# Two pairs of heads share one group of value products; first weights and the planner's costs changed

## The chip, the cores and the metric

The kernel runs on one core of one Trainium2 chip. The metric is the device time of one execution in microseconds. Before the change three runs gave 741.05, 739.51 and 741.62 us, so the median is 741.05.

## What is computed

Attention over 4 batches, 8 heads, 768 positions and 64 columns a head, followed by a gated feed-forward layer over all 3072 tokens. A query sees the 96 positions up to itself and the first 8 positions of its batch; a bias that grows with the distance is added to the scores.

```python
scores = scale * q @ k.T + bias            # per batch and head, 768 x 768
scores = where(is_global | is_local, scores, -1e9)
a = exp(scores - max(scores)); a = a / (sum(a) + 1e-9)
x = (a @ v), heads side by side            # 3072 x 512
out = ((x @ w_a) * (x @ w_b)) @ w_out      # 512 -> 1536 twice, product, 1536 -> 512
```

## The kernel before

**Units.** The 24 blocks of 128 queries are cut into eight units of 4, 2, 3, 3, 3, 3, 3 and 3 blocks. While PE does the feed-forward layer of one unit (`moe`), the attention of the next unit is made beside it (`attention`; for unit 0 `first`, for unit 1 `second`). Attention writes x, the layer's input, transposed: four chunks of 128 rows, one for each pair of heads.

**The feed-forward layer.** Every factor is split into a high and a low half, and a product is three matmuls: high by high, high by low, low by high. For each of twelve slices f of the 1536 columns, `proj` makes two such products into the banks p0 and p1 (L990, four chunks of x each; 384 columns wide in a unit of three blocks), the two are multiplied (L1029) and split (hh, hl), and `back` adds the product with the third weight to one accumulator a block (acc, L1008, 512 columns).

**Attention of units 2 to 7.** Heads are taken in pairs. For each head `split` makes the scaled query's halves qh and ql and the key's halves in kk. A block's scores are two matmuls, qh and ql, into one PSUM bank (L915); banks psS and psT took turns. DVE reads the bank, adds the bias and finds the maximum (L617), ACT takes the exponential (L633), DVE the sum and its reciprocal, ACT or DVE scales (L665, L667). DVE transposes the probabilities in squares of 32 by 32 into a staging tile in wm (L709), and when the pair is complete 16 small DMAs, on the queues of SP and ACT, put the squares in their places in pf (`swap`). Then PE multiplies pf by the values v: matmuls of 64 by 128, one group for each pair, into a bank pa (`values`, L742), and `result` copies pa to x. One row of L742 in PE's order stands for two matmuls of the trace. There are four such groups in a unit, 24 in units 2 to 7. pf has one buffer, so a pair's squares can land only when the group of the pair before is through.

**Units 0 and 1.** Here `quad` does two blocks of a pair of heads: a scaled query qs (L772 on ACT or L774 on DVE), scores (L789), softmax, transposes on PE (L692) that ACT or DVE copies to pf, and the same `values`.

**Weights.** The weights come as 24 pieces of 768 KB (`load_w`), two for each slice f, in a packed form of 64 bits a number. DMAs on SP's queue bring them to wr; ACT (L461, L498) and DVE (L468, L478, L488, L507) turn each into a float in wm; a copy (L419, L421) writes the high half wt, a subtraction (L429) the low half.

**The order.** No order is written by hand. Every step is an op with a due time, a cost on each engine that may do it, and the buffers that it reads and writes. `Schedule.order` plays the program through: at each moment an engine that is free takes the ready op with the earliest due time for which its buffers are free. `Schedule.search` repeats this with due times shifted at random for the ops due before the end of unit 1, and keeps a trial that ends sooner. The order of every engine, and of the loads on SP's queue, is what comes out. An engine then runs its instructions strictly in that order, each waiting by semaphores for what it needs.

Of the kernel before, what the change touches and what calls it, by code (L numbers as in the profile page):

```python
# [13 lines left out]
F32 = mybir.dt.float32  # L14
F32R = mybir.dt.float32r
# [8 lines left out]
B, H, S, D = 4, 8, 768, 64  # L24
DM, DFF = 512, 1536
P = 128
NB = S // P
NCC = DM // P
# [11 lines left out]
CHUNKS = 12  # L40
SQ = 32

SHORT = PAIRED
OLD = ()

START = 52000
WLEAD = 6000
# [6 lines left out]
SPARE = 200.0  # L54
# [3 lines left out]


TRIES = 400  # L60
SHARE = 0.03
SPREAD = 4000.0
# [82 lines left out]
MAXQ = max(p.nb for p in PLANS[1:]) * P  # L145
# [69 lines left out]
class Schedule:  # L215
# [22 lines left out]
    def search(self, limit, tries, share, spread):  # L238


        rnd = random.Random(1)
        ops = [op for op in self.ops if op.due < limit]
        dues = {op.index: op.due for op in ops}
        best = self.order(ops, dues)[1]
        for _ in range(tries):
            trial = dict(dues)
            for op in ops:
                if rnd.random() < share:
                    trial[op.index] += rnd.gauss(0.0, spread)
            end = self.order(ops, trial)[1]  # L250
            if end < best:
                best, dues = end, trial
        return self.order(self.ops, {op.index: dues.get(op.index, op.due) for op in self.ops})

    def order(self, ops, dues):
# [11 lines left out]
        out = []  # L267
        now = 0.0
        port = 0.0

# [29 lines left out]
        while len(out) < len(ops):  # L300
            started = True
            while started:
                started = False
                for e in free:
# [19 lines left out]
                    out.append(op)  # L324
                    free[e] = now + op.costs[e]
# [27 lines left out]
        return out, now  # L353
# [21 lines left out]
class Fast:  # L375
# [61 lines left out]
    def load_w(self, f, due):  # L437
# [3 lines left out]
        for g in range(2):  # L441
# [12 lines left out]
                due,  # L454
# [109 lines left out]
    def split(self, u, h, due, raw):  # L564
# [8 lines left out]
        ql = self.sbuf([P, MAXQ], F32R, "ql", "ql" + n, 2)  # L573
# [157 lines left out]
    def values(self, due, pl, blocks, v, probs, pa):  # L731


        nc = self.nc

        def emit(e):
            for i in blocks:
                slots = pl.vslot[i]
                for c, slot in enumerate(slots):
                    for s in range(2):  # L740
                        v0 = (s * pl.nv + slot) * D
                        nc.tensor.matmul(  # L742
                            pa[D * s : D * s + D, i * P : i * P + P],
                            v[:, v0 : v0 + D],
                            probs[s, i][1](c),
                            start=c == 0,
                            stop=c == len(slots) - 1,
                        )

        reads = [v] + [probs[s, i][0] for s in range(2) for i in blocks]  # L750
        n = sum(len(pl.vslot[i]) for i in blocks)
        self.plan.op(due, emit, reads, [pa], pe=n * 218 + 290, spare=SPARE if pl.late else 0.0)

    def quad(self, u, c, j, due, raw, v, pa, homes):
# [64 lines left out]
        self.values(due, pl, blocks, v, probs, pa)  # L819
        return pa  # L820

    def first(self, end):
# [14 lines left out]
        loads = [self.fetch_first(c, -1e6 + 2 * c) for c in range(NCC)]  # L837
# [36 lines left out]

    def result(self, u, c, due, pa, x):
# [11 lines left out]
    def attention(self, u, start, end):  # L887
        nc, pl, op = self.nc, PLANS[u], self.plan.op

        x = [(self.raw0, WIDE + c * MAXQ) for c in range(2)]  # L890
        x += [(self.sbuf([P, MAXQ], F32, f"x{c}", f"x{u}_{c}"), 0) for c in range(2, NCC)]
        if u < PAIRED:
            self.second(x, start, end)
            return x
        step = (end - start) / H
        for c in range(NCC):
            probs = {}
            v = self.fetch_v(u, c, start + (2 * c + 1) * step - LOADLEAD)
            pf = self.sbuf([P, CHUNKS * P], F32, "pf", f"pf{u}_{c}", 1)
            slot = 0  # L900
            old = u == SHORT and c in OLD
            for s in range(2):
# [4 lines left out]
                for i in range(pl.nb):  # L907
# [3 lines left out]
                    ps = self.bank(("psS", "psT")[not old and (pl.nb * h + i) % 2], "ps" + n)  # L911
# [37 lines left out]
            pa = self.bank("psA", f"pa{u}_{c}")  # L949
            self.values(due, pl, range(pl.nb), v, probs, pa)  # L950
            self.result(u, c, due, pa, x)
# [116 lines left out]
    def run(self):  # L1068
# [20 lines left out]
        order, end = self.plan.search(t2, TRIES, SHARE, SPREAD)  # L1089
# [376 lines left out]
```

## Time and profile before

| what | value |
|---|---|
| median of three runs | 741.05 us (739.51 to 741.62) |
| profiled execution | 739.72 us, of which the profile's span is 737.9 |
| mean granted TensorE clock | 0.994 |
| busy time of PE, DVE, ACT | 715.4, 480.0, 348.8 us |
| value products (L742), 640 matmuls | 43.7 us busy, 2.9 idle before them |
| scores of units 2 to 7 (L915), 288 matmuls | 77.9 us busy, 0.5 idle before them |
| weights loaded | 24 times 768 KB on SP's queue |

PE is TensorE's matmuls, PEld its weight loads, DVE VectorE, ACT ScalarE, SP SyncE. Busy times of PE overlap: a matmul starts before the one ahead of it is through, and its end is modelled. The distance between the starts of two matmuls therefore says more of PE's pace than the length of one. A row of the timeline gives the start, the time until the end of the last matmul in it, engine, line, what is written and read, the shape and the number of instructions; in brackets stands idle time ahead of it and what ended it. PEclk is the granted clock, 1.00 being full speed.

### The profile page before, as it was taken

To read this page: it belongs to the slowest core of one execution; us is meant where nothing else is said; L and a number is where in the kernel's file an instruction comes from. 1 tells how busy PE (TensorE), PEld (TensorE's weight loads), DVE (VectorE), ACT (ScalarE), POOL (GpSimd) and SP (SyncE) were. 2 spreads that over 40 slices of the span, in tenths; PEclk is the share of its full clock that TensorE was granted. 3 is DMA by queue.
4 is the path that set the end of the run, shared out by engine and by line. 5 is a ranking of instruction groups with operands and counts; after the bars stand their busy time and mean duration, and the time that the engine had idled before them with its cause. 6 is when DMAs were issued, how large, how long until landed. Compare 5 with 4: busy or idle time off the path is not lost.

```text
span 737.9 us, 12581 instructions
## 1 busy us (share of the span) xinstructions
PE 715.4 (97%) x4344; PEld 640.1 (87%) x4344; DVE 480.0 (65%) x1574; ACT 348.8 (47%) x891; POOL 8.9 (1%) x28
## 2 busy tenths in 40 slices
PE   5789999999999999999999999999999999999996
PEld 4567877889988999999999999999999999899996
DVE  5999999958956776287744878268672876321111
ACT  6999967556335353254424544154432544331112
POOL 1000000000000000000000000000000000000000
PEclk9999999999999999999999999999999999999999
DMA  7898211123533234124231443214341242110001
GB/s 282 345 339 326 82 32 33 35 85 110 142 106 113 84 98 116 44 83 110 74 116 44 108 122 96 73 61 107 88 128 55 81 127 62 47 44 0 1 1 47
DMA packets 38520, 74.58 MB, mean 101 GB/s; under 512 B 8496, under 2 KB 21040, under 8 KB 38448
## 3 DMA queue, kind: packets, MB, share of 16 engines
q1 hardware_dynamic: 29232, 65.03, 27.6%
q10 hardware_dynamic: 9216, 8.66, 4.6%
q8 instruction: 36, 0.59, 0.3%
q14 instruction: 36, 0.29, 0.1%
HBM read 50.07 MB, written 6.29 MB: 76 GB/s over the span
## 4 chain that ended last, share of the span: by engine, by line
PE 92%; DVE 4%; ACT 2%; DMA 1%; issue 0%; DVEq 0%; ACTq 0%; SPq 0%
PE p L990 54%; PE acc L1008 27%; PE pa L742 5%; PE ps L915 4%; PE ps L789 2%; DVE t L617 1%; PE pt L692 1%; DMA v<-qkv 0%; DMA nv<-ns 0%; DMA raw<-qkv 0%; DVE kk L429 0%; DVE t L667 0%; ACT kk L419 0%; ACT xh L419 0%; ACT wr L498 0%
## 5 line engine op out<-in xcount | busy, mean ns | idle before, releaser
L990 PE MATMUL p<-xh,wt 128*128 128x384 f32 (+2 forms) x1488 | 418.3, 338 | 1.1 <-DVE wt L429 0.6
L990 PEld LDWEIGHTS p<-xh,wt 128*128 128x128 f32 x1488 | 270.3, 188 | 15.3 <-issue 3.4
L990 PE MATMUL p<-xl,wt 128*128 128x384 f32 (+2 forms) x816 | 270.1, 341 | 0.3 <-DVE xl L429 0.3
L1008 PE MATMUL acc<-wt,hh 128*128 128x512 f32 x576 | 202.5, 394 | 0.0
L990 PEld LDWEIGHTS p<-xl,wt 128*128 128x128 f32 x816 | 153.9, 189 | 10.1 <-issue 1.0
L1008 PEld LDWEIGHTS acc<-wt,hh 128*128 128x128 f32 x576 | 108.2, 188 | 20.5 <-issue 1.3
L1029 DVE TENSOR_TENSOR raw<-p,raw 128x384 f32<-128x384 f32 (+2 forms) x96 | 52.9, 551 | 96.6 <-PE p L990 93.1
L1008 PE MATMUL acc<-wt,hl 128*128 128x512 f32 x288 | 113.1, 393 | 0.0
L633 ACT ACTIVATE t<-t,sm 128x232 f32<-128x232 f32 (+2 forms) x120 | 56.5, 472 | 93.9 <-DMA pf<-wm 77.6
L419 ACT COPY raw<-p 128x384 f32<-128x384 f32 (+2 forms) x84 | 39.9, 475 | 104.1 <-PE p L990 101.5
L1008 PEld LDWEIGHTS acc<-wt,hl 128*128 128x128 f32 x288 | 54.2, 188 | 7.6
L429 DVE TENSOR_TENSOR hl<-raw,hh 128x384 fp32r<-128x384 f32 (+2 forms) x95 | 52.1, 548 | 12.7 <-ACT hh L419 12.0
L617 DVE CUSTOM_DVE_ANT_0 t<-ps,rel 128x232 f32<-128x232 f32 (+1 forms) x100 | 38.1, 397 | 25.6 <-PE ps L915 23.2
L419 ACT CAST hh<-raw 128x384 fp32r<-128x384 f32 (+2 forms) x69 | 35.5, 515 | 39.2 <-DVE raw L1029 33.0
L742 PEld LDWEIGHTS pa<-pf,v 128*64 128x64 f32 x640 | 35.5, 138 | 13.0 <-issue 7.4
L742 PE MATMUL pa<-pf,v 128*64 128x128 f32 x640 | 43.7, 280 | 2.9 <-ACT pf L419 1.3
L633 ACT ACTIVATE wm<-wm,sm 128x232 f32<-128x232 f32 (+2 forms) x72 | 34.0, 472 | 23.8 <-DVE sm L617 20.1
L429 DVE TENSOR_TENSOR kk<-raw,kk 64x348 fp32r<-64x348 f32 (+1 forms) x90 | 41.6, 463 | 2.8
L915 PE MATMUL ps<-kk,ql 128*128 128x232 f32 (+2 forms) x144 | 39.4, 275 | 0.0
L915 PE MATMUL ps<-kk,qh 128*128 128x232 f32 (+2 forms) x144 | 38.5, 270 | 0.5 <-DVE sm L617 0.4
L665 ACT ACTIVATE wm<-wm,sm 128x232 f32<-128x232 f32 (+2 forms) x58 | 27.5, 478 | 23.3 <-DVE sm L655 21.0
L709 DVE STREAM_TRANSPOSE wm<-wm 128x256 f32<-128x256 f32 (+1 forms) x72 | 29.6, 414 | 6.7 <-ACT wm L665 5.7
(87 smaller groups left out, 666.8 us busy)
## 6 DMA issues: line engine op xcount, KB each, us to landing
wr<-wts SPq DMA_DIRECT2D x24, 768.0 KB, 10.8
raw<-qkv SPq DMA_DIRECT2D x24, 366.0 KB, 3.1
raw<-qkv SPq DMA_DIRECT2D x24, 314.0 KB, 2.9
v<-qkv SPq DMA_DIRECT2D x16, 384.0 KB, 3.1
out<-o SPq DMA_DIRECT2D x23, 256.0 KB, 2.1
pf<-wm SPq DMA_DIRECT2D x96, 48.0 KB, 2.0
pf<-wm ACTq DMA_DIRECT2D x96, 48.0 KB, 2.0
v<-qkv SPq DMA_DIRECT2D x16, 256.0 KB, 2.7
```

The costliest lines, as they stand in the source:

```text
L419: self.nc.scalar.copy(out(), src())
L429: lambda e: self.engine(e).tensor_sub(out(), a(), b()),
L617: lambda e, j=j, o=o, w=w, neg=neg: nc.vector.tensor_tensor_reduce(t[:, o : o + w], ps[:, o : o + w], neg[:, :w], -(2.0 ** -(h + 1)), 3.0e ...
L633: lambda e, j=j, o=o, w=w: nc.scalar.activation(t[:, o : o + w], t[:, o : o + w], AF.Exp, bias=sm[:, j : j + 1], scale=-1.0, accum_out=sm[ ...
L665: nc.scalar.mul(t[:, o : o + w], t[:, o : o + w], r)
L709: nc.vector.transpose(dst, src)
L742: nc.tensor.matmul(pa[D * s : D * s + D, i * P : i * P + P], v[:, v0 : v0 + D], probs[s, i][1](c), start=c == 0, stop=c == len(slots) - 1,)
L789: nc.tensor.matmul(ps[s][:, o : o + w], qs[r, q0 + m * P : q0 + m * P + P], raw[r, kc : kc + w], start=True, stop=True,)
L915: nc.tensor.matmul(ps[:, :w], q[:, i * P : i * P + P], kk[:, k0 : k0 + w], start=m == 0, stop=m == 1,)
L990: nc.tensor.matmul(p[:, :T], wt(), b[:, b0 : b0 + T], start=c == 0 and n == 0, stop=c == NCC - 1 and n == 2,)
L1008: nc.tensor.matmul(acc[i][:, :], hs[:, i * P : i * P + P], wt(), start=f == 0 and n == 0, stop=f == NF - 1 and n == 2,)
L1029: lambda e, asb=asb, pb=pb: nc.vector.tensor_mul(asb[:, :T], pb[:, :T], asb[:, :T]),
```

## The change

**Pairs joined.** `values` takes a list of pairs, and `attention` hands it two at a time. So a unit of 2 to 7 has two groups in place of four, each with twice the matmuls; the first pair writes the bank psA, the second psT. psT is thus no longer free for scores, and all scores of these units go to psS. pf has two buffers, and x's second half (chunks 2 and 3) lies in pf's buffers where it had tiles of its own; it is taken only behind the unit's first group. ql has one buffer where it had two. `result` of both pairs comes behind the joined group.

**First weights sooner.** The loads of the two pieces of f = 0, and those of the first unit's queries, keys and values, get due times that interleave them. On SP's queue stood, behind the first pair's loads, raw_1, v_1, raw_2, v_2, raw_3, v_3 and only then the weights; now stands the first piece of weights, raw_1, v_1, the second piece, raw_2, v_2, raw_3, v_3, and further weights.

**The planner.** `order` also adds up the time that PE waits beyond 1.3 us in one place, doubled and at most 1.3 us a place, and `search` minimises the sum of this and the end. It makes 1200 trials in place of 400, and in each shifts fewer due times (1% in place of 3%) by more (8 us in place of 4). It reorders nothing by a rule; but every order of units 0 and 1, and what follows from it, may differ.

```diff
+JOINT = 2
+EARLY = -60000
+LOAD = 4000
+IDLE = 1300.0
+FINE = 2.0
-TRIES = 400
-SHARE = 0.03
-SPREAD = 4000.0
+TRIES = 1200
+SHARE = 0.01
+SPREAD = 8000.0
...
 def search(self, limit, tries, share, spread):
-        best = self.order(ops, dues)[1]
+        best = self.order(ops, dues)[1:]
...
-            end = self.order(ops, trial)[1]
-            if end < best:
-                best, dues = end, trial
+            found = self.order(ops, trial)[1:]
+            if sum(found) < sum(best):
+                best, dues = found, trial
...
 def order(self, ops, dues):
...
+                    if e == "pe":
+                        fine += min(max(now - free[e] - IDLE, 0.0) * FINE, IDLE)
...
 def load_w(self, f, due):
-                due,
+                EARLY + (2 * g + 1) * LOAD if f == 0 else due,
                 lambda e, f=f, g=g, raw=raw: nc.sync.dma_start(...),
...
 def split(self, u, h, due, raw):
-        ql = self.sbuf([P, MAXQ], F32R, "ql", "ql" + n, 2)
+        ql = self.sbuf([P, MAXQ], F32R, "ql", "ql" + n)
...
-    def values(self, due, pl, blocks, v, probs, pa):
+    def values(self, due, pl, blocks, groups):
         def emit(e):
-            for i in blocks:
+            for v, probs, pa in groups:
+                for i in blocks:
...
+        for v, probs, pa in groups:
+            reads += [v] + [probs[s, i][0] for s in range(2) for i in blocks]
+            writes.append(pa)
+        n = len(groups) * sum(len(pl.vslot[i]) for i in blocks)
+        self.plan.op(due, emit, reads, writes, pe=n * 218 + 290, ...)
...
 def first(self, end):
-        loads = [self.fetch_first(c, -1e6 + 2 * c) for c in range(NCC)]
+        loads = [self.fetch_first(c, EARLY + 2 * c * LOAD) for c in range(NCC)]
...
+    def probs32(self, name):
+        return self.sbuf([P, CHUNKS * P], F32, "pf", name, JOINT)
...
 def attention(self, u, start, end):
-        x += [(self.sbuf([P, MAXQ], F32, f"x{c}", f"x{u}_{c}"), 0) for c in range(2, NCC)]
...
-            pf = self.sbuf([P, CHUNKS * P], F32, "pf", f"pf{u}_{c}", 1)
+            pf = self.probs32(f"pf{u}_{c}")
...
-                    ps = self.bank(("psS", "psT")[not old and (pl.nb * h + i) % 2], "ps" + n)
+                    ps = self.bank("psS", "ps" + n)
...
-            pa = self.bank("psA", f"pa{u}_{c}")
-            self.values(due, pl, range(pl.nb), v, probs, pa)
-            self.result(u, c, due, pa, x)
+            pa = self.bank(("psA", "psT")[c % JOINT], f"pa{u}_{c}")
+            groups.append((v, probs, pa))
+            if len(groups) == JOINT:
+                self.values(due, pl, range(pl.nb), groups)
+                if len(x) <= c:
+                    x += [(self.probs32(f"x{u}_{k}"), 0) for k in range(2, NCC)]
+                for k, (_, _, pa) in enumerate(groups, c + 1 - JOINT):
+                    self.result(u, k, due, pa, x)
+                groups = []
```

Behind the inserted code the lines have moved: L742 is L755 in the changed kernel, L915 is L936, L990 is L1017, L1008 is L1035.

Three places in the orders. The first is on PE, where unit 4's first values are multiplied. A name such as pa4_0 is unit 4's pair 0; acc3 and p03 are the feed-forward layer of unit 3; the number behind the last underscore only tells buffers apart. Before:

```order
L1008 MATMUL acc3_0_3656<-wt2_1_767,hh3_2_3754 128x512
L1008 MATMUL acc3_0_3656<-wt2_1_767,hl3_2_3761 128x512
L1008 MATMUL acc3_0_3656<-wt2_1_767,hh3_2_3754 128x512
L742 MATMUL pa4_0_3843<-pf4_0_3742,v4_0_3312 64x128 x10
L1008 MATMUL acc3_1_3662<-wt2_1_767,hh3_2_3754 128x512
L1008 MATMUL acc3_1_3662<-wt2_1_767,hl3_2_3761 128x512
```

And in the changed kernel:

```order
L936 MATMUL ps4_5_0_4026<-kk4_5_3890,qh4_5_3883 128x128
L936 MATMUL ps4_5_0_4026<-kk4_5_3890,ql4_5_3977 128x128
L1017 MATMUL p03_6_4032<-xh3_3505,wt6_0_1094 128x384
L1017 MATMUL p03_6_4032<-xl3_3513,wt6_0_1094 128x384
L1017 MATMUL p03_6_4032<-xh3_3505,wt6_0_1094 128x384
L755 MATMUL pa4_0_4037<-pf4_0_3749,v4_0_3448 64x128 x10
L755 MATMUL pa4_1_4048<-pf4_1_3936,v4_1_3455 64x128 x10
L1017 MATMUL p03_6_4032<-xh3_3505,wt6_0_1094 128x384
```

The products of pair 0 have moved back to those of pair 1, and nothing stands between them. The rows before them are those of slice 6 where they were of slice 2.

The second place is on PE too, where unit 5's first scores are made (ps5_0_1 is unit 5, head 0, block 1). Before:

```order
L915 MATMUL ps5_0_0_4554<-kk5_0_4228,qh5_0_4211 128x232
L915 MATMUL ps5_0_0_4554<-kk5_0_4228,ql5_0_4219 128x232
L915 MATMUL ps5_0_1_4558<-kk5_0_4228,qh5_0_4211 128x232
L915 MATMUL ps5_0_1_4558<-kk5_0_4228,ql5_0_4219 128x232
L990 MATMUL p04_1_4564<-xh4_4489,wt1_0_635 128x384
L990 MATMUL p04_1_4564<-xl4_4497,wt1_0_635 128x384
L990 MATMUL p04_1_4564<-xh4_4489,wt1_0_635 128x384
L915 MATMUL ps5_0_2_4570<-kk5_0_4228,qh5_0_4211 128x232
```

And in the changed kernel:

```order
L936 MATMUL ps5_0_0_4550<-kk5_0_4224,qh5_0_4213 128x232
L936 MATMUL ps5_0_0_4550<-kk5_0_4224,ql5_0_4297 128x232
L1017 MATMUL p04_1_4557<-xh4_4485,wt1_0_646 128x384
L1017 MATMUL p04_1_4557<-xl4_4493,wt1_0_646 128x384
L1017 MATMUL p04_1_4557<-xh4_4485,wt1_0_646 128x384
L936 MATMUL ps5_0_1_4563<-kk5_0_4224,qh5_0_4213 128x232
L936 MATMUL ps5_0_1_4563<-kk5_0_4224,ql5_0_4297 128x232
```

The first two blocks' scores stood side by side, in two banks. Now one product of the feed-forward layer, three matmuls, stands between any two, and all of them write the one bank psS.

The third place is the end of unit 0's attention. Before, ACT had there (xl_332 takes the high half of the last chunk of x, qs_0_0 is unit 1's first scaled query):

```order
L419 COPY pf_0_3_1_602<-pt_0_3_1_583 128x512
L419 COPY pf_0_3_1_608<-pt_0_3_1_597 128x512
L498 ACTIVATE wr_1_384<-wr_1_384 128x768
L498 ACTIVATE wr_1_451<-wr_1_451 128x768
L461 ACTIVATE wm<-wr_0_422 128x768
L419 CAST xl_332<-pa_3_564 128x512
L419 CAST wt_0_635<-wm 128x768
L772 ACTIVATE qs_0_0_638<-raw_0_550,sc 128x256
```

In the changed kernel that query is on DVE, whose order has at this place:

```order
L678 TENSOR_SCALAR t_0_3_1_507<-t_0_3_1_507,sm_0_3_1_508 128x232
L678 TENSOR_SCALAR t_0_3_1_524<-t_0_3_1_524,sm_0_3_1_525 128x232 x2
L790 TENSOR_SCALAR qs_0_0_593<-raw_0_550,sc 128x256
L479 TENSOR_SCALAR wm<-wm 128x768 x2
L489 TENSOR_SCALAR wm<-wm 128x768 x2
L499 SCALAR_TENSOR_TENSOR wm<-wr_0_356,wm 128x768
L499 SCALAR_TENSOR_TENSOR wm<-wr_1_393,wm 128x768
L518 ISA wm<-wr_0_356,wm 128x1536
L865 TENSOR_TENSOR xl_3_644<-pa_3_566,xl_301 128x512
```

The scaled query has moved from behind the cast of x on ACT to ahead of the weights' steps and of the low half of x (xl_3) on DVE.

More of the change, by code (lines that the diff above doesn't have):

```diff
@@ L269, in order @@
         port = 0.0
+        fine = 0.0
         def arrive(op):
@@ L352, in order @@
                         live[b.tag] -= 1
-        return out, now
+        return out, now, fine
 def act(n, psum=False):
@@ L729, in swap @@
                 )
-    def values(self, due, pl, blocks, v, probs, pa):
+    def values(self, due, pl, blocks, groups):
         nc = self.nc
         def emit(e):
-            for i in blocks:
[L738 to L752, printed above, removed]
+            for v, probs, pa in groups:
+                for i in blocks:
+                    slots = pl.vslot[i]
+                    for c, slot in enumerate(slots):
+                        for s in range(2):
+                            v0 = (s * pl.nv + slot) * D
+                            nc.tensor.matmul(
+                                pa[D * s : D * s + D, i * P : i * P + P],
+                                v[:, v0 : v0 + D],
+                                probs[s, i][1](c),
+                                start=c == 0,
+                                stop=c == len(slots) - 1,
+                            )
+        reads, writes = [], []
+        for v, probs, pa in groups:
+            reads += [v] + [probs[s, i][0] for s in range(2) for i in blocks]
+            writes.append(pa)
+        n = len(groups) * sum(len(pl.vslot[i]) for i in blocks)
+        self.plan.op(due, emit, reads, writes, pe=n * 218 + 290, spare=SPARE if pl.late else 0.0)
     def quad(self, u, c, j, due, raw, v, pa, homes):
@@ L818, in quad @@
             pa = self.bank("psS", f"pa{n}")
-        self.values(due, pl, blocks, v, probs, pa)
+        self.values(due, pl, blocks, [(v, probs, pa)])
         return pa
@@ L890, in attention @@
         x = [(self.raw0, WIDE + c * MAXQ) for c in range(2)]
-        x += [(self.sbuf([P, MAXQ], F32, f"x{c}", f"x{u}_{c}"), 0) for c in range(2, NCC)]
         if u < PAIRED:
+            x += [(self.probs32(f"x{u}_{c}"), 0) for c in range(2, NCC)]
             self.second(x, start, end)
@@ L948, in attention @@
                 self.swap(due, pf, slot)
-            pa = self.bank("psA", f"pa{u}_{c}")
-            self.values(due, pl, range(pl.nb), v, probs, pa)
-            self.result(u, c, due, pa, x)
+            pa = self.bank(("psA", "psT")[c % JOINT], f"pa{u}_{c}")
[6 more added lines that the diff above has]
+                    self.result(u, k, due, pa, x)
+                groups = []
         return x
@@ L1088, in run @@
             t += NF * steps[u]
-        order, end = self.plan.search(t2, TRIES, SHARE, SPREAD)
+        order, end, _ = self.plan.search(t2, TRIES, SHARE, SPREAD)
         if TRACE:
```

## The prediction

> **What bounds the kernel now.** I read the page first, for the busy engine and the chain that ended last.
>
> ```profile
> span 737.9 us, 12581 instructions
> PE 715.4 (97%) x4344; PEld 640.1 (87%) x4344; DVE 480.0 (65%) x1574; ACT 348.8 (47%) x891; POOL 8.9 (1%) x28
> ...
> PE   5789999999999999999999999999999999999996
> ...
> DVE  5999999958956776287744878268672876321111
> ...
> PE 92%; DVE 4%; ACT 2%; DMA 1%; issue 0%; DVEq 0%; ACTq 0%; SPq 0%
> ```
>
> PE is busy for 97% of the span and carries 92% of the chain. Only about 22 us are open at all (737.9 less 715.4), and the slices show where: the first three or four, and the end. DVE is full from the second slice to the eighth and half empty later. The second view is the busy time by stretch.
>
> ```profile
> core 0: us, PE busy (x) PEld busy (x) DVE busy (x) ACT busy (x) POOL busy (x), PEclk, DMA share, GB/s
> 0.00:20.00 20.00, 12.37 (x91) 9.27 (x93) 12.58 (x77) 13.48 (x43) 2.04 (x19) 0.91 0.78 292
> ...
> 40.00:60.00 20.00, 17.00 (x82) 12.69 (x81) 18.45 (x35) 18.98 (x34) 0.00 (x0) 0.91 0.93 349
> ...
> 80.00:100.00 20.00, 20.00 (x102) 16.03 (x101) 20.00 (x37) 15.22 (x24) 0.00 (x0) 1.00 0.04 14
> ...
> 200.00:250.00 50.00, 48.81 (x331) 44.18 (x329) 31.86 (x115) 22.88 (x63) 2.02 (x2) 1.00 0.37 106
> ...
> 600.00:650.00 50.00, 49.50 (x317) 45.51 (x316) 27.24 (x95) 17.97 (x50) 0.00 (x0) 1.00 0.24 64
> ```
>
> Two regimes follow. Up to about 100 us DVE decides (20.00 of 20 us): it turns weights into two halves while it does the first softmaxes. From there PE alone decides, and time is won only by taking work or gaps out of PE's own line. Where PE has no idle time (600 to 650 us lacks 0.50), a gap must be looked for in the distance between the starts of matmuls, since a busy PE may be spaced wider than it need be. So the third view is PE's timeline around one group of products with the values, here one with 512-column matmuls on both sides.
>
> ```profile
> 349.12 0.40 PE L1008 MATMUL acc<-wt,hh 128*128 128x512 f32 x1
> 349.45 1.31 PE L742 MATMUL pa<-pf,v 128*64 128x128 f32 x20
> 350.69 0.50 PE L1008 MATMUL acc<-wt,hh 128*128 128x512 f32 x1
> 351.03 0.40 PE L1008 MATMUL acc<-wt,hl 128*128 128x512 f32 x1
> 351.27 0.39 PE L1008 MATMUL acc<-wt,hh 128*128 128x512 f32 x1
> ```
>
> **Part 1, pairs joined.** In this fence a 512-column matmul takes 0.24 us to the next start (351.03 to 351.27). Into the group it takes 0.33, so 0.10 more; the first one behind the group takes 0.34, again 0.10 more. The group itself takes 1.24 us for 20 recorded matmuls. Units of three full blocks have 24:
>
> ```profile
> 436.45 1.53 PE L742 MATMUL pa<-pf,v 128*64 128x128 f32 x24
> 437.91 0.37 PE L915 MATMUL ps<-kk,qh 128*128 128x232 f32 x1
> ```
>
> That is 1.46 us, so four matmuls are worth 0.22, twenty 1.10, and 0.14 of a group's time is its own fixed part. One group thus costs 0.10 + 0.14 + 0.10 = 0.34 us beyond its products. The change leaves all products and takes away 12 of 24 groups (units 2 to 7, four pairs each): 12 x 0.34 = **-4.1 us**. All of it lies on PE, which nothing covers there.
>
> What could take this back is the start of a group's second half. Each pair's first product waits for eight DMA queues, which PE's sequencer handles as four separate waits. Before, these stand ahead of long matmuls; now four of them stand between short ones.
>
> ```profile
> L742 PEldq EVENT_SEMAPHORE  x4: 51/51/51, 348.7 to 349.0; - x4
> ...
> L742 PEld LDWEIGHTS pa<-pf,v x16: 133/137/137, 642.8 to 643.5; 128*64 128x64 f32 x16
> ...
> L742 PEldq EVENT_SEMAPHORE  x4: 51/126/1029, 639.5 to 641.0; - x4
> ```
>
> The first row is the group at 349.45: four waits take about 0.4 us and end 0.4 us ahead of it, hidden. In the other two rows the sequencer is 1.8 us ahead (641.0 to 642.8). Inside a group the matmuls ahead of it are worth 1.10 to 1.32 us, more than 0.4, so I price the middle at 0. The bounds are 0 and 12 x 0.4 = 4.8 us, if the sequencer has no lead there; nothing makes it cheaper than 0. The Trainium skill, "TensorE: Matmul & The Clock Gate", section "Engine queue depths", gives PE's queue 64 places; by that the sequencer could hold the whole first half, and the price is 0, where the first row's lead alone (0.4 us) would leave up to half of it open. The traces here show no lead longer than a few microseconds, so neither row proves the depth.
>
> **Part 2, late data.** A group that comes before its transposed probabilities have landed leaves PE idle:
>
> ```profile
> L742 PE MATMUL pa<-pf,v 128*64 128x128 f32 x640 | 43.7, 280 | 2.9 <-ACT pf L419 1.3 <-issue 1.0 <-PE p L990 0.5
> ...
> 627.42 0.34 PE L990 MATMUL p<-xl,wt 128*128 128x384 f32 x1
> 627.59 0.34 PE L990 MATMUL p<-xh,wt 128*128 128x384 f32 x1
> 628.43 1.53 PE L742 MATMUL pa<-pf,v 128*64 128x128 f32 x24 [0.50 <-PE p L990]
> ```
>
> Of 2.9 us, 1.3 belong to the first unit, whose pf ACT writes; at most 1.6 are late groups. In a joined group the first half was ready a pair earlier, and the second starts 1.1 us or more behind the group's start. I take **-0.7**, between 0 and -1.6.
>
> **Part 3, one bank for scores.** All scores of units 2 to 7 now share psS, where two banks took turns, so each waits until DVE has read the one before. Behind that wait stands everything on PE. How fast DVE answers:
>
> ```profile
> 219.31 0.28 PE L915 MATMUL ps<-kk,ql 128*128 128x232 f32 x1
> 219.62 0.40 DVE L617 CUSTOM_DVE_ANT_0 t<-ps,rel 128x232 f32<-128x232 f32 x1 [2.76 <-PE ps L915]
> 219.89 0.27 PE L915 MATMUL ps<-kk,ql 128*128 128x232 f32 x1
> 220.30 0.27 PE L915 MATMUL ps<-kk,ql 128*128 128x232 f32 x1
> 220.53 0.38 DVE L617 CUSTOM_DVE_ANT_0 wm<-ps,rel 128x232 f32<-128x232 f32 x1
> 220.98 0.38 PE L915 MATMUL ps<-kk,qh 128*128 128x232 f32 x1 [0.41 <-DVE sm L617]
> ```
>
> A free DVE is done 0.71 us after the second score matmul starts (219.31 to 220.02); a busy one let the bank go so that PE went on 1.09 us after it (219.89 to 220.98). In the new order most scores have far more work between them, but at the start of units 4 to 7 only three 384-column matmuls: 3 x 0.17 (627.42 to 627.59) and about 0.10 for the score's own second matmul (an estimate, 0.17 x 232/384), 0.61 us. So each of four places waits 0.1 to 0.5 us. Ten more have six matmuls, 1.12 us, just enough. I take **+0.9**, four times 0.15 and 0.3 for unit 2, where DVE is busier; bounds 0 and +3. The single ql buffer (two before) is written in the same gaps, and is in this price.
>
> **Part 4, the start.** The first matmuls with weights are held up by one hole.
>
> ```profile
> 41.75 1.57 PE L742 MATMUL pa<-pf,v 128*64 128x128 f32 x16
> 46.27 1.79 PE L789 MATMUL ps<-raw,qs 64*128 64x232 f32 x8 [2.95 <-ACT qs L772]
> 47.98 2.51 PE L990 MATMUL p<-xl,wt 128*128 128x512 f32 x6
> ...
> 44.48 0.59 ACT L419 CAST xl<-pa 128x512 fp32r<-128x512 f32 x1
> ...
> 45.37 0.68 DVE L849 TENSOR_TENSOR xl<-pa,xl 128x512 fp32r<-128x512 f32 x1
> ...
> 11.43 0.35 DVE L774 TENSOR_SCALAR qs<-raw,sc 128x256 f32<-128x256 f32 x1
> ...
> 8.00:20.00 12.00, 9.99 (x81) 7.02 (x79) 9.26 (x58) 10.59 (x39) 0.00 (x0) 0.86 1.02 413
> 46.30:50.30 4.00, 4.00 (x14) 2.72 (x14) 2.75 (x6) 2.98 (x5) 0.00 (x0) 0.57 0.99 346
> ```
>
> PE idles 2.95 us for a scaled q that ACT makes behind the cast of the last x, and then runs 4 us at a clock of 0.57, which costs another 4.0 x 0.43 = 1.7. Now DVE makes that q long before the cast, so PE does those scores in the hole and goes on about 0.2 us behind the cast's end (45.07): some 1.2 us of hole are left, 1.7 are gone, and with them probably the slow clock. That is 3.4 us at PE. But DVE is the limit until 100 us, so what stays is what DVE gains: it idled 4.00 - 2.75 = 1.25 us behind that hole, and that goes. Earlier, weights fill DVE's gaps (12.00 - 9.26 = 2.7 us between 8 and 20 us), but the first 768 KB of weights now pass ahead of the second pair's q and k on SP's queue, 1.9 us at 413 GB/s, and the scaling at 11.43 us, which did not wait, will. I set these two against each other: **-1.3**, between +1 and -3.5.
>
> **Part 5, from unit 1 to unit 2.** In 200 to 250 us PE lacks 1.19 us, most of it where unit 2 starts. Now the last joined group and two output triples stand between the last product of unit 1 and the first of unit 2, so the casts of the first half of x run under them; but both late chunks of x come from that group. I take **-0.6**, between -1.2 and +1.2.
>
> **The sum.** -4.1 - 0.7 + 0.9 - 1.3 - 0.6 = -5.8 us. The profiled execution took 739.7 us (span and 1.8 around it), which gives 733.9. It lies 1.3 below the median of the three runs (741.05; 739.51 to 741.62), half their scatter; I add 0.6 for a median: **734.5 us**.
>
> **The rivals.**
>
> DVE holds the start (chance 0.25). DVE's 20.00 of 20 us speaks for it: PE comes early to the next weights and waits. Parts 4 and 5 give nothing, or the late q costs 1: -3.9 to -2.9, so 736.4 to 737.4.
>
> The start gives all (0.12). Nothing holds PE later: -3.5 there and -1.2 at the boundary make -8.6, 731.7. Against it speaks the same row.
>
> The group is joined in name only (0.08). The sequencer has no lead in the middle, and four waits of 0.1 us there cost 0.35 or more each time: part 1 falls to about 0, the rest is -1.7, 738.6 to 740, within what can be told from no change: I use 0.3%, 2.2 us, as about what a measurement of this kernel can resolve. For it: the waits take 0.4 us wherever they stand. Against: the lead of 1.8 us.
>
> One bank slows the clock (0.05). Each short wait for psS lets the clock fall for 4 us, at 1.7 us a time. The fourteen close places could cost 24; six make it slower than before (6 x 1.7 = 10.2 against 5.8, 745 us), fewer do not. For it: the hole at 43 us did just that. Against: PE waited for a bank at 220.98, and the clock of 200 to 250 us is 1.00. The Trainium skill, "TensorE: Matmul & The Clock Gate", section "A second HAM failure mode: psum-queue depth-cycling", describes a matmul kernel that cycles PSUM banks and lets PE idle briefly so often that its clock swings between half and full. By that rule this rival comes true; the trace here shows one such wait without it.
>
> **How the numbers follow.** The forecast has 0.50 and spans 733 to 736 with the sizes of its terms. Faster by over 0.3% (below 738.8) are the forecast and the first two rivals: 0.50 + 0.25 + 0.12 = 0.87. The joined-in-name case is the 0.08 of no change, the clock the 0.05 of slower. From 730.5 to 738.8 lie the forecast, the first rival and most of the second, a little over 8 in 10.
>
> **What would show it.** Part 1 is right if a joined group of 40 takes about 2.34 us (2 x 1.10 + 0.14), with no extra gap at its middle; 2.7 would be the third rival. Part 2: idle time before pa from unit 2 on below 1 us. Part 3: PE waits on DVE's score reads of a few tenths at the starts of units 5 and 7; over 3 us in all would be wrong, and so would any PEclk below 0.98 after 100 us. Part 4: the idle time near 43 us below 1.5 us, PEclk of 40 to 60 us at 1.00, and the stretches to 100 us with DVE still full. The forecast is wrong if the stretch from 310 us to the end is not about 3 us shorter.

## The result, and the profile after

The changed kernel takes 733.88 us (median of six runs, 733.24 to 735.12), the kernel before 741.51 (six runs, 739.51 to 741.96). The ratio of the means is 0.9903, with a 95% interval of 0.9889 to 0.9917. The forecast was 734.5. The profiled execution took 733.24 us, its span is 731.5, 6.4 less than before.

The total was right, but in part by luck: terms of its working were off both ways, and the rest of this document is about that. First the page of the changed kernel: its span, the busy engines, the chain, and the rows of the value products (L755, L742 before) and of the scores (L936, L915 before).

```profile
span 731.5 us, 12548 instructions
PE 710.8 (97%) x4344; PEld 639.2 (87%) x4344; DVE 478.0 (65%) x1575; ACT 348.4 (48%) x894; POOL 6.6 (1%) x24
...
PE 86%; DVE 6%; ACT 4%; DMA 2%; ACTq 1%; issue 1%; DVEq 0%
...
L755 PE MATMUL pa<-pf,v 128*64 128x128 f32 x640 | 40.4, 279 | 0.3 <-ACT pf L430 0.3
L936 PE MATMUL ps<-kk,qh 128*128 128x128 f32 (+1 forms) x144 | 39.0, 271 | 1.4 <-DVE sm L628 1.2
```

The idle time ahead of the value products has gone from 2.9 to 0.3 us. Ahead of the scores it has grown from 0.5 to 1.4, and the chain has more of DVE and ACT in it than before. Next the busy time by stretch.

```profile
core 0: us, PE busy (x) PEld busy (x) DVE busy (x) ACT busy (x) POOL busy (x), PEclk, DMA share, GB/s
0.00:20.00 20.00, 11.13 (x75) 8.20 (x75) 12.62 (x69) 14.10 (x41) 2.05 (x19) 1.00 0.78 295
...
40.00:60.00 20.00, 18.05 (x94) 13.78 (x93) 19.93 (x40) 20.00 (x36) 0.00 (x0) 1.00 0.97 369
...
80.00:100.00 20.00, 20.00 (x100) 15.98 (x99) 20.00 (x30) 13.32 (x19) 0.00 (x0) 1.00 0.06 14
...
200.00:250.00 50.00, 50.00 (x324) 46.38 (x323) 36.70 (x132) 23.88 (x67) 0.00 (x0) 1.00 0.35 101
...
400.00:450.00 50.00, 48.96 (x306) 45.38 (x305) 40.14 (x152) 22.27 (x67) 0.00 (x0) 1.00 0.39 107
```

Three things differ from before. The clock is 1.00 from 40 to 60 us, where it was 0.91. (The first stretch shows 1.00 too, but there the trace has no clock record for the first 14.85 us; the last section comes back to this.) From 200 to 250 us PE has no hole left. And from 400 to 450 it has a new one, of 1.04 us, where the kernel before had none. DVE is at least as full as before (19.93 and 20.00 of 20 us).

Where the time came from is read best from the same piece of work in both traces. Unit 3's feed-forward layer begins with its first product, and the last slice of unit 7 begins with another. Before:

```profile
307.68 0.34 PE L990 MATMUL p<-xh,wt 128*128 128x384 f32 x1
...
723.55 0.34 PE L990 MATMUL p<-xh,wt 128*128 128x384 f32 x1
```

In the changed kernel:

```profile
301.70 0.34 PE L1017 MATMUL p<-xh,wt 128*128 128x384 f32 x1
...
717.29 0.34 PE L1017 MATMUL p<-xh,wt 128*128 128x384 f32 x1
```

At unit 3 the changed kernel is already 5.98 us ahead, at the end 6.26. Between the two, where eight of the twelve joined groups stand, it gained 0.3. The prediction said that it would be wrong if this stretch were not about 3 us shorter.

To see more, I took for every matmul the distance to the start of the next one, less the usual distance of its kind (medians over both traces: 0.233 us for 512 columns of L990, 0.174 for 384, 0.117 for 256, 0.230 for L1008, 0.109 for a score of 232 columns; for a value matmul the mean within a group, 0.055). The usual distances add up to 691.2 us of work in every kernel here; what is left over is PE's loss. It is 34.8 us before and 28.4 after, and the difference is the 6.4 of the spans. By stretches of work (in the kernel before, work of 30 us is reached at 54 us, 140 at 167, 230 at 262, 650 at 690). Behind 650 nothing is lost in either. The forecast's terms are put where they belong: three of the twelve joins lie from 140 to 230, nine behind.

| work, us | what it holds | before | after | change | forecast |
|---|---|---|---|---|---|
| 0 to 30 | unit 0's attention, first slices | 18.3 | 15.7 | -2.5 | -1.3 |
| 30 to 140 | unit 0's layer, first of unit 1's | 3.0 | 3.1 | +0.1 | 0 |
| 140 to 230 | rest of unit 1's layer, first half of unit 2's | 5.2 | 2.3 | -2.9 | -1.5 |
| 230 to 650 | the layers behind it, attention of units 3 to 7 | 8.5 | 7.4 | -1.1 | -3.0 |

(The forecasts are 3 x 0.34 for joins, 0.2 of the late data and 0.6 of part 5, less 0.3 for the bank; and 9 x 0.34 and 0.5, less 0.6.) In the last row the value groups and their neighbours lose 4.09 us less (7.55 to 3.46), where 3.6 was forecast, and scores with the three matmuls behind them 2.87 us more (0.76 to 3.63), where 0.6 was. So the forecast held because the start and the boundary gave 2.6 us more than it said, the late data 0.5 more, and the one bank took 2.3 more.

### The profile page after: what moved, and what is told of

Read it like the earlier page. It is cut to its first block, busy times and chain, and to the rows that moved or that the text cites. A ratio compares the mean times of both kernels' runs of the same rounds, so it can differ in the third digit from the quotient of the medians.

```text
span 731.5 us, 12548 instructions
## 1 busy us (share of the span) xinstructions
PE 710.8 (97%) x4344; PEld 639.2 (87%) x4344; DVE 478.0 (65%) x1575; ACT 348.4 (48%) x894; POOL 6.6 (1%) x24
## 4 chain that ended last, share of the span: by engine, by line
PE 86%; DVE 6%; ACT 4%; DMA 2%; ACTq 1%; issue 1%; DVEq 0%
PE p L1017 50%; PE acc L1035 25%; PE pa L755 5%; PE ps L936 4%; ACT t L644 1%; ACTq L734 1%; DMA pf<-wm 1%; PE ps L805 1%; DVE wm L720 1%; DVE kk L440 1%; PE pt L703 1%; ACT pf L430 1%; DVE t L628 1%; ACT wr L509 1%; ACT wm L472 0%
## 5 line engine op out<-in xcount | busy, mean ns | idle before, releaser
L1017 PE MATMUL p<-xh,wt 128*128 128x384 f32 (+2 forms) x1488 | 419.1, 338 | 2.9 <-ACT raw L430 1.3
L1017 PEld LDWEIGHTS p<-xh,wt 128*128 128x128 f32 x1488 | 270.5, 188 | 16.4 <-issue 2.6
L1017 PE MATMUL p<-xl,wt 128*128 128x384 f32 (+2 forms) x816 | 269.4, 340 | 0.7 <-DVE xl L865 0.4
L1035 PE MATMUL acc<-wt,hh 128*128 128x512 f32 x576 | 202.5, 394 | 0.0
L1017 PEld LDWEIGHTS p<-xl,wt 128*128 128x128 f32 x816 | 153.3, 188 | 10.1 <-ACT xl L430 0.7
L1035 PEld LDWEIGHTS acc<-wt,hh 128*128 128x128 f32 x576 | 108.2, 188 | 19.7 <-issue 0.5
L1035 PE MATMUL acc<-wt,hl 128*128 128x512 f32 x288 | 113.0, 393 | 0.0
L430 ACT COPY raw<-p 128x384 f32<-128x384 f32 (+2 forms) x70 | 34.5, 492 | 90.9 <-PE p L1017 90.7
L1035 PEld LDWEIGHTS acc<-wt,hl 128*128 128x128 f32 x288 | 54.2, 188 | 7.5
L430 ACT CAST hh<-raw 128x384 fp32r<-128x384 f32 (+2 forms) x76 | 39.8, 523 | 35.4 <-DVE raw L1056 35.3
L440 DVE TENSOR_TENSOR kk<-raw,kk 64x348 fp32r<-64x348 f32 (+1 forms) x93 | 43.1, 463 | 2.9
L644 ACT ACTIVATE wm<-wm,sm 128x232 f32<-128x232 f32 (+2 forms) x72 | 33.9, 471 | 14.1 <-DVE sm L628 13.8
L755 PE MATMUL pa<-pf,v 128*64 128x128 f32 x640 | 40.4, 279 | 0.3 <-ACT pf L430 0.3
L936 PE MATMUL ps<-kk,qh 128*128 128x128 f32 (+1 forms) x144 | 39.0, 271 | 1.4 <-DVE sm L628 1.2
L755 PEld LDWEIGHTS pa<-pf,v 128*64 128x64 f32 x640 | 35.3, 138 | 5.8 <-issue 4.2
L936 PE MATMUL ps<-kk,ql 128*128 128x128 f32 (+1 forms) x144 | 39.6, 275 | 0.0
L676 ACT ACTIVATE wm<-wm,sm 128x232 f32<-128x232 f32 (+2 forms) x53 | 25.2, 480 | 17.3 <-DVE sm L666 16.1
L430 ACT COPY x<-pa 128x384 f32<-128x384 f32 (+1 forms) x14 | 6.5, 464 | 55.6 <-PE pa L755 55.6
```

Of the source, the lines that this page charges most:

```text
L430: self.nc.scalar.copy(out(), src())
L440: lambda e: self.engine(e).tensor_sub(out(), a(), b()),
L644: lambda e, j=j, o=o, w=w: nc.scalar.activation(t[:, o : o + w], t[:, o : o + w], AF.Exp, bias=sm[:, j : j + 1], scale=-1.0, accum_out=sm[ ...
L676: nc.scalar.mul(t[:, o : o + w], t[:, o : o + w], r)
L755: nc.tensor.matmul(pa[D * s : D * s + D, i * P : i * P + P], v[:, v0 : v0 + D], probs[s, i][1](c), start=c == 0, stop=c == len(slots) - 1,)
L936: nc.tensor.matmul(ps[:, :w], q[:, i * P : i * P + P], kk[:, k0 : k0 + w], start=m == 0, stop=m == 1,)
```

## The experiments

Each kernel was timed against the kernel before on the same chip, and profiled once. Three chips were used for them, with medians of 741.33 to 741.67 us for the kernel before, so between two kernels the ratios say a little more than the times. Executions of some kernels here scatter by 2 to 7 us, so the profiled one can lie off its median: by 2.4 us at worst, in the kernel with pairs joined alone. Sums by stretch come from that one execution, and they scatter too. The kernel before was profiled twice: the two traces lose 18.3 and 18.3 us up to 30 us of work, 5.2 and 6.3 from 140 to 230, 8.5 and 9.1 from 230 to 650. Four kernels share the changed kernel's order up to unit 3's scores: they lose 15.7, 16.8, 16.8 and 15.6 us at the start, and 1.9 to 2.3 from 140 to 230. So a difference of about 1 us in one stretch is no more than chance may make. The theories: A, read from the two traces, says that the one bank is dear and the start and boundary are worth more than forecast; B is the prediction's own terms; C is named where it stands.

**The new loads and the new search, without joined pairs.** The kernel before with the loads, the trials and the charge for long waits of the change:

```diff
+EARLY, LOAD, IDLE, FINE = -60000, 4000, 1300.0, 2.0
+TRIES, SHARE, SPREAD = 1200, 0.01, 8000.0
...
```

> The kernel before with the new loads and the new search alone; pairs stay apart and scores keep two banks. Theory A (read from the two traces): the start gives 2.5 us and part of the way from unit 1 to unit 2 another 0 to 2, so 737 to 739 us; from unit 3 on the matmuls lie as before, with four groups a unit. Theory B (the terms as predicted): 1.3 and at most 0.6, so 739.5 to 740.2. Theory C (the start's gain in the trace was the chance of a clock): no change, 741 to 742.

Measured 735.22 us, ratio 0.9920 (0.9908 to 0.9932): 6.3 us of the change's 7.6 are here without one joined pair. It is more than any theory gave. By stretches it loses 15.4, 2.6, 3.3 and 7.8 us: 2.9 won at the start, 1.9 at the boundary.

**Joined pairs alone.** The changed kernel with the old loads and the old search:

```diff
-TRIES, SHARE, SPREAD, FINE = 1200, 0.01, 8000.0, 2.0
+TRIES, SHARE, SPREAD, FINE = 400, 0.03, 4000.0, 0.0
-                EARLY + (2 * g + 1) * LOAD if f == 0 else due,
+                due,
...
-        loads = [self.fetch_first(c, EARLY + 2 * c * LOAD) for c in range(NCC)]
+        loads = [self.fetch_first(c, -1e6 + 2 * c) for c in range(NCC)]
```

> The changed kernel with the old search and the old loads, so that joining the pairs stands alone. Theory A: groups -4.2, late data -1.2, waits for the one bank +4.0, so about 740 us (739 to 741), little or nothing gained. Theory B (as predicted): -4.1 - 0.7 + 0.9, so 737.6. In the trace A wants some 3 to 4 us of distances ahead of and behind scores that wait for DVE, B about 1.

Measured 736.71 us, ratio 0.9935 (0.9917 to 0.9953), so B's sum fits better than A's. By stretches 17.3, 2.7, 3.6, 5.9. From work 230 on it wins 2.6 us: the value groups the same 4.09 as in the changed kernel, and scores and what is behind them lose 1.33 more than before, not 2.87. The one bank's price is thus not fixed. Alone, the two halves of the change give 6.3 and 4.8 us, together 7.6: both improve the same places, the start and the boundary.

**Scores in two halves of one bank.** The two halves of psS take turns, 256 columns each:

```diff
...
+            self.home = self.bank("psS", "psH")
...
-                    ps = self.bank("psS", "ps" + n)
+                    half = (pl.nb * h + i) % 2
+                    ps, p0 = self.home, 256 * half
...
-                                ps[:, :w],
+                                ps[:, p0 : p0 + w],
...
```

> The changed kernel, but the scores of units 2 to 7 take turns in the two halves of the bank psS (256 columns each), so that PE can write one while DVE reads the other. Theory A: the waits for the bank, 4.0 us in all and 3.0 of them from unit 3 on, go away: 730 to 731 us, and PE no longer waits on DVE ahead of scores. Theory B: only 0.9 to win, 733. A rival to both: PE and DVE in the same bank hold each other up, then DVE's reads get longer than 0.40 us or the distances at scores stay, 734 or more.

Measured 746.32 us, ratio 1.0066 (1.0053 to 1.0079), 12.4 above the changed kernel. The planner put scores as close as two buffers allow, but the program's waits hold for the whole tile. In this kernel's timeline:

```profile
408.06 0.27 PE L938 MATMUL psH<-kk,qh 128*128 128x232 f32 x1
...
408.94 0.39 DVE L628 CUSTOM_DVE_ANT_0 wm<-psH,rel 128x232 f32<-128x232 f32 x1
409.25 0.08 DVE L628 DVE_READ_ACCUMULATOR2_ANT sm<- 128x1 f32 x1
...
409.39 0.38 PE L938 MATMUL psH<-kk,qh 128*128 128x232 f32 x1 [0.42 <-DVE sm L628]
```

The score at 409.39 goes into the other half than that of 408.06, and yet starts only when DVE has read that of 408.06 (409.25 + 0.08). DVE's read still takes 0.39 us. PE wrote nothing into the bank meanwhile, so whether the two engines would hold each other up there is not shown; what holds the score back here is a wait in the program. This kernel shows what many such waits cost. The answer on the scores' line, from 225 us on:

```profile
L938 PE MATMUL psH<-kk,qh x112: 217/271/389, 237.7 to 636.6; 128*128 128x232 f32 x80, 128*128 128x128 f32 x16, 128*128 128x256 f32 x16
...
  DVE sm L628: 19.3, 44
...
250.00:300.00 50.00, 48.18 (x321) 43.39 (x321) 28.39 (x99) 17.71 (x49) 0.71 (x1) 1.00 0.37 102
```

44 times PE or its weight loads sat idle for DVE's read, and scores and their neighbours lose 13.2 us. The clock stays at 1.00 in this stretch, the one from 225 us on in which PE is idle most.

**The kernel before once more.** No edit.

> The kernel before, unchanged, profiled once more. If the slow clock behind the hole at 43 us (0.57 for 4 us) belongs to this kernel, it stands there again, and the stretch 40 to 60 us shows about 0.91. If it is chance, the clock there is 1.00 or the dip lies elsewhere, and the time stays within its usual scatter of 739.5 to 742 us.

Its one run took 741.73 us. The two stretches with the slow clock are there again:

```profile
0.00:20.00 20.00, 12.26 (x91) 9.29 (x93) 12.48 (x75) 13.52 (x43) 2.05 (x19) 0.91 0.77 293
...
40.00:60.00 20.00, 16.98 (x82) 12.78 (x82) 18.40 (x36) 19.17 (x33) 0.00 (x0) 0.91 0.93 349
```

The loss up to 30 us of work is the same to 0.01 us (18.26). So the slow clock at 46 us belongs to this order of the work. The four traces with the changed kernel's start all show 1.00 from 40 to 60 us, so taking it away was a gain that lasts.

**Two banks for three of four heads.**

```diff
-                    ps = self.bank("psS", "ps" + n)
+                    ps = self.bank(("psS", "psT")[h % 4 > 0 and i % 2], "ps" + n)
```

> The changed kernel, but the scores of every head other than the first of two joined pairs (three of four heads) take turns in psS and psT again; psT is free for them because the group before them has already been read. Theory A: the one bank costs 4.0 us in the changed kernel, 2.9 of it from unit 3 on, and about 1.6 of that stands at these heads: 732 to 732.5 us, with about half the distances ahead of scores left. Theory B (as predicted, 0.9 in all): 733.3 to 733.9. Theory C (from the experiment with two halves): PE is let closer to DVE and waits more often: 735 or more.

Measured 735.92 us, ratio 0.9921 (0.9904 to 0.9938), 2.0 above the changed kernel, which ran on another chip, where A wanted 1.5 below. The late stretch did what A said: it loses 6.1 instead of 7.4 us, scores and neighbours 2.2 instead of 3.6. But unit 2's scores are among the ops that the search moves, so it found another start: 17.9 and 4.2 us where the changed kernel has 15.7 and 2.3. An edit that is to be priced here must leave the search's ops alone.

**The loads alone, and the search alone**, both on the kernel before.

> The kernel before with the earlier first loads alone (old search). The planner and the loads together gave 6.3 us. Theory A: the start's gain comes from the first weights standing ahead of the later queries and keys: the stretch to 100 us of work gives some 2.5 of it, so 738.5 to 739 us. Theory B: the loads only change which draw of the search is found; then the time may lie anywhere from 735 to 742 and the gain isn't at the start.

> The kernel before with the new search alone (1200 trials, long waits charged), old loads. Theory A: the search gives what stands from unit 1 to unit 2, some 2 us, and little at the start: 739 to 740 us. Theory B: the search is what found the better start, and the loads nothing: 735 to 737.

Loads: 737.51 us, ratio 0.9942 (0.9922 to 0.9961). Search: 737.84 us, ratio 0.9951 (0.9934 to 0.9967). By stretches the loads lose 15.3, 2.7, 8.0 and 8.0 us, the search 16.4, 2.6, 3.4 and 9.8. So A's idea of the loads is right for the start (3.0 won), but without the new search their draw has a hole behind (2.8 lost from 140 to 230: PE waits 2.13 us at 214 us, and then runs for 3.4 us at half the clock). The search wins in both places, more than A said, and B's claim that the loads do nothing falls. Neither alone is worth what the two are together.

**The changed kernel without the charge for long waits** (FINE = 0.0).

> The changed kernel with long waits of PE not charged (factor 0 in place of 2); its search minimises the end alone. Theory A: the charge matters little, since PE's waits at the start are covered by DVE, which decides up to 100 us: 733 to 735 us. Theory B: it removes holes that let the clock fall (1.7 us each): then one or two come back and it takes 735.5 to 737.5, with a PEclk below 0.95 in a stretch up to 60 us.

Measured 734.00 us, ratio 0.9897 (0.9881 to 0.9914): the charge makes no difference that can be told. Neither from 20 to 40 nor from 40 to 60 us is the clock below 1.00. That A's sum came true does not prove its reason: DVE does not cover PE's waits there, as is shown below.

**Joined or apart, one bank or two, with the same start.** Three kernels have the changed kernel's order word for word up to unit 3's scores, and differ from there on. Pairs apart, two banks:

```diff
+            joint = JOINT if u == PAIRED else 1
-            pa = self.bank(("psA", "psT")[c % JOINT], f"pa{u}_{c}")
+            pa = self.bank(("psA", "psT")[c % joint], f"pa{u}_{c}")
...
-                    ps = self.bank("psS", "ps" + n)
+                    ps = self.bank(("psS", "psT")[u > PAIRED and (pl.nb * h + i) % 2], "ps" + n)
```

> The changed kernel with its own order up to unit 3's scores, but from unit 3 on every pair has its group for itself again and the scores take turns in psS and psT. Theory A (by stretches of the traces so far): the groups cost 3.4 and their late data 0.7 more, the scores 2.9 less: 1.2 us more than the changed kernel, about 735. Theory B (terms as predicted): 3.4 + 0.6 - 0.75 = 3.2 us more, 737.

Pairs apart, one bank: the same without the last edit.

> As the one before it, pairs apart from unit 3 on, but all scores in the one bank psS as in the changed kernel. Theory A: the bank costs the same 2.9 us whether pairs are joined or not, so this is 4.1 above the changed kernel, 738. Theory C: the bank by itself costs 1.3 us, and the rest was one long wait (1.1 us at 417.6) that comes of how DVE's order fell in the changed kernel: 736 to 736.6.

Pairs joined, and from unit 3 on three of four heads in two banks:

```diff
+                    ps = self.bank(("psS", "psT")[u > PAIRED and h % 4 > 0 and i % 2], "ps" + n)
```

> The changed kernel with its own order up to unit 3's scores, pairs joined, and from unit 3 on the scores of three of four heads in two banks. Theory A: the waits ahead of these scores go, 1.5 us less than the changed kernel: 732.4. Theory B (as predicted, the bank cost 0.9 in all): 733.3 or more, not to be told from the changed kernel.

| from unit 3 on | median, us | ratio (interval) | loss from work 230 to 650 | value groups | scores and next three |
|---|---|---|---|---|---|
| joined, one bank (the change) | 733.88 | 0.9903 (0.9889 to 0.9917) | 7.4 | 3.46 | 3.63 |
| apart, two banks | 735.27 | 0.9927 (0.9907 to 0.9948) | 8.2 | 7.04 | 0.78 |
| apart, one bank | 737.79 | 0.9955 (0.9937 to 0.9974) | 10.6 | 8.59 | 1.80 |
| joined, mostly two banks | 733.06 | 0.9894 (0.9874 to 0.9913) | 5.5 | 3.39 | 1.70 |

The same answer on the scores' line from 225 us on carries the last column. Joined, one bank:

```profile
L936 PE MATMUL ps<-kk,qh x117: 218/270/383, 225.2 to 624.0; 128*128 128x232 f32 x85, 128*128 128x128 f32 x16, 128*128 128x256 f32 x16
...
  DVE sm L628: 4.6, 9
```

Apart, two banks, where no wait for DVE is left:

```profile
L936 PE MATMUL ps<-kk,qh x117: 218/269/374, 226.4 to 626.7; 128*128 128x232 f32 x85, 128*128 128x128 f32 x16, 128*128 128x256 f32 x16
...
  issue: 1.0, 6
```

Joined, mostly two banks:

```profile
L936 PE MATMUL ps<-kk,qh x117: 222/269/377, 225.1 to 621.7; 128*128 128x232 f32 x85, 128*128 128x128 f32 x16, 128*128 128x256 f32 x16
...
  DVE sm L628: 0.6, 3
```

Joining is worth 3.1 us with one bank (10.6 to 7.4) and 2.7 with two (8.2 to 5.5). The bank costs 2.4 us apart, and 1.9 joined against a kernel that keeps it for one head in four. What the change did there, both at once, is 0.7 us in these traces, less than they scatter, and 1.4 in the medians, whose intervals overlap. A's 735 and 738 were met (735.27, 737.79); that C's 736 to 736.6 was not, though the scores lose only 1.0 more there, is because the rest went to late groups (8.59 against 7.04). The last kernel is the fastest median of the study, but its interval contains most of the changed kernel's: that it beats it is not shown by the times, only its late stretch is 2.0 us shorter in the one execution profiled.

**The kernel before with another draw** (`random.Random(2)`).

> The kernel before, its old loads and its old search, with another seed of the random numbers (2 in place of 1). Theory A: what the start and the way from unit 1 to unit 2 cost is a matter of the draw, and the kernel before had a poor one: 737 to 740 us. Theory B: the new loads and search found what the old can't: 741 to 742.5.

Measured 740.59 us, ratio 0.9992 (0.9978 to 1.0007), not to be told from the kernel before. By stretches 19.1, 2.6, 3.7 and 9.2: the other draw is 1.5 us better at the boundary; that it is worse at the start and late, by 0.9 and 0.7, is no more than the scatter. Two draws don't make a distribution, but that the kernel before merely had a poor one is not borne out.

## Why the prediction was right in its sum and wrong in its working

**Part 1, pairs joined, was right.** A joined group of 40 recorded matmuls in the changed kernel:

```profile
343.32 0.34 PE L1017 MATMUL p<-xh,wt 128*128 128x384 f32 x1
343.59 2.40 PE L755 MATMUL pa<-pf,v 128*64 128x128 f32 x40
345.92 0.44 PE L1017 MATMUL p<-xh,wt 128*128 128x384 f32 x1
346.20 0.33 PE L1017 MATMUL p<-xl,wt 128*128 128x384 f32 x1
```

From its start to that of the next matmul it takes 2.33 us; 2.34 was forecast. The four waits in its middle cost nothing, so "joined in name only" falls. With the start held the same, nine of the twelve joins bring 3.65 us at the value groups (7.04 to 3.39); 9 x 0.34 = 3.1 of it is their own price, the rest late data.

**Part 2, late data, had the right size.** Idle time ahead of the value products is down by 2.6 us, but 1.7 of that lies before 45 us (2.0 to 0.3). From unit 2 on it goes from 0.9 us to nothing, so the prediction's bound of 1.6 was too wide, and its mark, below 1 us from unit 2 on, was met before the change already. By the distances between starts it is 1.2 us: the four late groups (0.30, 0.23, 0.10 and 0.57 us late, at 216, 296, 523 and 628 us) are gone. 0.7 was taken.

**Part 3, one bank for scores, was mis-sized: +0.9 forecast, +2.9 from unit 3 on alone.** The step that failed is "I take +0.9, four times 0.15 and 0.3 for unit 2". It priced DVE as free or busy with one instruction, and looked for the bank's waits where scores stand close. At the starts that it named, no score of the changed kernel waits longer than 0.03 us. The dearest wait stands where fifteen matmuls of 384 columns lie between two scores. DVE's order there, and PE beside it:

```profile
416.63 1.10 DVE L720 STREAM_TRANSPOSE wm<-t 128x256 f32<-128x256 f32 x3 [0.95 <-DMA pf<-wm]
417.65 0.52 DVE L440 TENSOR_TENSOR hl<-raw,hh 128x384 fp32r<-128x384 f32 x1
418.09 0.44 DVE L720 STREAM_TRANSPOSE wm<-wm 128x256 f32<-128x256 f32 x1
418.45 0.36 DVE L628 CUSTOM_DVE_ANT_0 wm<-ps,rel 128x232 f32<-128x232 f32 x1
...
417.62 0.34 PE L1017 MATMUL p<-xh,wt 128*128 128x384 f32 x1
418.88 0.38 PE L936 MATMUL ps<-kk,qh 128*128 128x232 f32 x1 [0.92 <-DVE sm L628]
```

DVE sat idle 0.95 us because the staging tile was still being emptied by the DMAs of the pair before, then did three transposes, a subtraction and a fourth transpose, and only then read the bank. PE went on 1.26 us after its last product, 1.09 more than usual. With two banks that score would have had the other one: in the kernel with mostly two banks the wait at this place, at 418.7 us, is 0.09 us. So the bank's price is set by what stands ahead of the read in DVE's order, a DMA included, not by the read's 0.4 us. At the scores and what follows them it was 1.0 us with pairs apart, 1.3 where joining stood alone, 1.9 against mostly two banks and 2.9 against the kernel before. The waits ahead of the scores alone are 2.0 of the 2.9 us, and 0.5 in unit 2; the rest is a slower start of the scores and matmuls behind. So the waits are nearly three times the 0.9 of the forecast, though 2.5 us does not pass the prediction's own mark of 3.

**Part 4, the start, was mis-sized: -1.3 forecast, -2.5 measured in the profiled execution, -1.5 to -2.7 in the four with this start.** The hole and the slow clock behind it went as described. PE's waits there in the changed kernel:

```profile
44.36 0.50 PE L1017 MATMUL p<-xl,wt 128*128 128x512 f32 x1 [0.33 <-ACT xl L430]
45.22 1.43 PE L1017 MATMUL p<-xl,wt 128*128 128x512 f32 x5 [0.36 <-DVE xl L865]
47.90 0.50 PE L1017 MATMUL p<-xh,wt 128*128 128x512 f32 x1 [1.25 <-ACT raw L430]
```

They are 1.94 us in place of 2.95 (more than the 1.5 of the prediction's mark), and the clock of the stretch is 1.00. What failed is the step "DVE is the limit until 100 us, so what stays is what DVE gains". DVE is full there, but PE does not wait for it: from 80 to 100 us PE is busy for 20.00 of 20 us in both kernels, and from work 30 to 140 it loses 3.0 and 3.1 us. A start that is 2.5 us ahead at 30 us of work stays so. The rival "DVE holds the start" had the same fault, and "the start gives all" (3.5 and 1.2 us) came about as near for these two places as the forecast did.

**Part 5, from unit 1 to unit 2, was mis-sized too: -0.6 forecast.** From work 140 to 230 the scores and the matmuls behind them lose 1.25 us instead of 2.85, 1.6 less (0.3 was forecast, the bank's share taken off), and unit 2's bank waits are already in that. The kernel with new loads and search alone wins 1.9 in this stretch and another draw of the old search 1.5, so most of it is the order's doing and not the joined group's.

**One bank slows the clock.** It did not: the changed kernel's clock is 1.00 in every stretch from 100 to 700 us, and in the kernel with two halves 44 waits, none above 0.8 us, didn't move it; no run of matmuls there starts at twice its usual distance. The Trainium skill, "TensorE: Matmul & The Clock Gate", section "A second HAM failure mode: psum-queue depth-cycling", describes a kernel in which short waits between groups of matmuls made the clock swing. Waits of 19.3 us in 44 places, spread over 400 us, did not do that here.

So the sum of -5.8 met -6.4 in the traces because 2.6 us too little at the start and the boundary, and 0.5 at the late data, stood against 2.3 too little for the bank (0.1 is left over between work 30 and 140, and roundings). That the errors cancelled is luck, and a total inside its range does not confirm its terms. By its own mark the forecast was wrong: the stretch from 310 us to the end is 0.3 us shorter, not 3.

## What to carry to other kernels

A shared buffer costs what stands ahead of its reader in the reader's queue, waits for DMAs included; count that, not the read's own length. An engine that is full is a bound only if another waits for it: look at the distances between PE's starts in the same stretch. And where a random search sets the order, an edit moves places that it does not touch, so compare variants that leave the searched part alone, and compare by pieces of work rather than by totals, after profiling one order more than once to see how far a piece scatters.

## What the runs showed of the hardware

A clock of 1.00 in a row need not be one that was recorded. The kernel before, at 10.81 us, and its clock behind that:

```profile
10.81 1.24 PE L692 MATMUL pt<-ident,t 128*128 128x128 f32 x6 [1.99 <-DVE sm L655]
...
13.00:16.00 3.00, 3.00 (x21) 2.39 (x20) 2.09 (x12) 1.79 (x8) 0.00 (x0) 0.55 1.03 417
```

The changed kernel at the same place, and matmuls of the same kind at 39.58 us:

```profile
10.85 1.51 PE L703 MATMUL pt<-ident,t 128*128 128x128 f32 x6 [1.92 <-DVE sm L666]
...
13.00:16.00 3.00, 3.00 (x24) 2.25 (x22) 1.88 (x6) 2.67 (x7) 0.00 (x0) 1.00 1.00 415
...
39.58 1.03 PE L703 MATMUL pt<-ident,t 128*128 128x128 f32 x8
```

It looks as if the clock fell after 1.99 us of idle time and stayed up after 1.92. It did not: at 10.85 us six transposes take 1.51 us, where eight take 1.03 at 39.58. They start 0.21 us apart, twice their usual 0.109. The changed kernel's trace has no clock record before 14.85 us, and the row shows 1.00 for that time; the records of the kernel before begin at 8.90 us, with half the clock from 12.31 to 15.72. In all fourteen traces a clock of 1.00 that then holds for 20 us or more begins only between 14.2 and 18.7 us.

Nor does the length of this wait tell the traces apart. With 1.85 us of it the kernel with the search alone has a record of the slow clock, and the one without the charge has none; with pairs joined alone it is 1.99 us, as before the change, and there is none either. What decides it stays open.

Later in the run PE's waits of 2.95 us (2.97 in the second trace) and of 2.13 us, in the kernel with the loads alone, are each followed by 3.4 us at half the clock. No other wait after 20 us is longer than 1.43 us. One more stretch at half the clock, from 38.3 to 41.7 us in the kernel with another draw, has no wait above 1.19 us ahead of it, so the length of one wait is not the whole rule.
